# Bilinear MLP, second sweep: the last pair of chunks by seven block products, and a new order table

## The chip, the cores and the metric

The kernel runs on one core of one Trainium2 chip. The metric is the device time of one launch in microseconds (us).

## The reference

```
a   = softmax(phi, over s)                    # phi: 4 x 8 x 576 x 32
k_m = einsum('bhsm,bhsd->bhmd', a, k);  v_m = einsum('bhsm,bhsd->bhmd', a, v)
x   = softmax(q @ k_m.T / 8) @ v_m            # -> 2304 tokens x 512
h   = x @ w_in                                # 512 x 2048
x   = max(0.01*h, h) @ w_out                  # 2048 x 512
out = ((x @ w_a) * (x @ w_b)) @ w_out2        # 512 x 1536, 512 x 1536, 1536 x 512
```

All in fp32. The two MLPs are called the first and the second below.

## The kernel before

Every large product is made of three TensorE passes over fp32r halves (PASSES: high by high, high by low, low by high), so each operand is split: a CAST on ACT (or DVE) makes the high half, a subtraction on DVE the low one.

**Head.** For each batch `b` and group `g` of heads, `kv_part` (L506) loads phi, k and v, takes the maximum of phi on DVE (`nmx`, L490) and the exponential on ACT (L496), transposes it on TensorE (`ta` L543, `tz` L546), copies it out (`en`, L365) and multiplies it with k and v (`km`, L562). The norm `kvn` (L578 on ACT, L580 on DVE) and a transpose `kvt` (L588) follow, and `kd` and `vm` are copied out of it. `sc` (L636) are the scores, `vw` (L719) is v_m by the first chunk of w_in, and `h` (L770) the first product of the first MLP. That chunk comes in four pieces (`raw_win`), which `weight` (L410) takes apart: `high` L429 and `low` L432 on ACT, then clamp L436, shift L440, join L444 and a last addition L447 on DVE. `idle` (L388) places four `warm` transposes (L392), whose result nobody reads, behind a named tile. The first 38 `warm` (L384) run before any data has come.

**Second MLP.** It runs in two sweeps `s` over 12 chunks `c` of 128 of the 1536 columns. `ab_unit` (L1045) makes both factors of one chunk by seven block products of six matmuls each, in three PSUM tiles `abx`, `aby`, `abz` (L1061); ACT copies between them (L1072) and DVE adds (L1069). Two adjacent chunks `2q`, `2q+1` are a pair, and the pair's product with w_out2 is done in one of two ways, as `by_seven(s, c)` (L1126) says from the table `SEVENS`:

- By `o_unit` (L1137): the factors are multiplied (L1093, L1096) and split into `p`. Eight units of six matmuls (L1158), each into a PSUM tile `o` of its own, are added on DVE to the sum `osum` (L1171). In the last pair the eighth unit is cut into 320 and 192 columns. In the last pair each unit is followed by its transfer to the output (L1179).
- By `o_part`: the factors go unsplit into `pf` (L1088, L1091). `p_sums` (L1220) makes T1 to T4 from the blocks B11, B12, B21, B22 by subtraction (L1229), and splits T1 to T4, B11, B21 and B22 into `pb` (CAST L365 on ACT, L1239 on DVE). `w2_sums` (L1185) loads that pair of chunks of w_out2 (L1190) and makes S1 to S4 and their splits from it (L1204, L1214). `o_part` (L1260) then has, for each of two halves `x`, seven parts of three matmuls of 512 columns (L1277). A part is called here by its right operand. B11, T2, T3 and T4 go one after the other into the same PSUM tile `os_x`; B21 goes into `os_y`; T1 and B22 go into `os_z`. After B11, T2 and T3 the running sum in `os_x` is copied out by ACT (`ok`, L1297). After the others DVE adds the tile to `osum` (L1311), and, but for T4, the matching `ok` too (L1314). In the last pair the transfer to the output follows (L1321).

**Order.** `Program.run` (L275) issues the operations in the order of the table `ORDER`: an operation's number, with a letter a (ACT) or v (DVE) where either could do it. Each engine works through its own share strictly in that order. `PLACES` names the buffer of each tile; the tiles `os_x` of all pairs lie in one PSUM bank, those of `os_y` and `os_z` in a second.

Of the kernel before, what the change touches and what calls it, by code (L numbers as in the profile page):

```python
# [58 lines left out]
SEVENS = ((0,1,2,3,8,9,10,11), tuple(range(10)))  # L59
# [30 lines left out]
24 246 0 4 238 1 26 25 224 27 3 28 2 247 29 31 30 231 248 249v 34a 250 32a 251 35 33 45 239 240 241v 23 252v 242 253 5 44 243 6 244v 22 36 7 8 46 226 37 10a  # L90
47 225 245 38v 227v 49 9 11 12a 39 65 13 40a 43v 41a 14 228 42a 232 48 229 15 64 16a 230v 233 17 234v 290 20a 235 21a 19a 18v 257 299 236 259a 237v 258a 87
88 89 254 75 50 255a 256a 76 63 90 51 77 52 91v 98 55 54 78 57a 92 53 66 79 56a 67 68a 93 150 69a 80v 116 58 94v 81 117 70 59v 95 101 82 291 60 326 292 61a
332 62v 115 71a 83v 300 328 327 293v 301 84 99 72 330 333 294 96a 302v 334 73a 295 100 329 74a 303 331 296v 139 85a 317 304 335 336 297a 140 102 308 265
305v 344 266a 168 103 141 267 268a 338 142 306a 127 345 269 337 143v 104 167 128 154 144 106 340 339a 145 155 342 108a 129 156 130 146v 158 131 343a 118 341
147 160a 119 364 121a 120a 132v 169 148a 105 86v 133 157 319 122 149v 318 134 153 260 320v 358 261a 123a 262 310 135v 263a 309 264 136 170 311v 124 151 172a
384 126v 137a 372 125a 138v 365a 107 312 159 390 179 109a 385 313 386 171 321 161a 391 110 314v 173a 373 322 359a 354 152 111a 323v 374 392 112 375v 348
113a 114v 315a 352 324a 316v 356 325v 355 349 387v 350 180 351v 393v 370 357v 298v 307v 181 360 97v 371a 353a 182 366 362 361 183 376 368 367 363v 184v 369v
185 174 377a 186 270 541 382 273a 271a 175a 272 187v 394 383a 274 188 176 532 346 178a 189a 177a 190v 395a 378 505 191 379 380 162 193 347a 192 194 275 550
195v 559 396 276a 278a 277 196 279 388 163a 197 542 414 381v 389a 198v 406 415 199 416 398 544v 200a 417v 164 201v 418 165a 166a 397 543 399v 545 407a 213
533 546 412 215 547v 214 548a 216 202 552 534 402 203 204 419a 217v 413a 408 561 205 403 280 409 206v 218 424 404 281a 405v 410 411v 432 425a 219 283a 436  # L100
434 207 282 208 285 437a 560 284 426 209v 433 288a 430 428 289 507 210 427 286a 211a 287 400 220v 431a 551 212v 420 221 442 429v 498 222a 535v 484 421 223v
491 422 423v 450 443a 435v 506 536 438 562v 451 537 452 444 401a 563 458 553v 446 453v 439 448 440 564 445 459 554 460 538v 441v 462 565v 447v 466 463 555
464 566a 454 556v 467 461v 472 468 455 456 478 557a 457v 567v 539a 470 499 549v 1274 492 1300 540v 1281 473 558v 479 449a 465v 474 469v 485 476 475v 486
508v 480 471a 481v 493 509 501v 500 494v 482 510 477a 1275 502 503 495 487v 496 572 483a 488 1276 489 1301 497v 1302 511v 490v 578 573a 504v 1277v 1303v 512
1278 579a 1304 1279 584 513a 515a 514 1305 590 1280v 516 1292a 1306v 585a 568 1293v 1307 1308a 1282 574 1310 1309v 1283 1284v 1314 522 569 1285 570 1286 575
580 576 1287v 591a 571v 586 581 1288v 1294a 577v 596 582 1289v 587 583v 588 1290v 1296a 1291v 589v 592 1298a 1297v 525a 598 593 1312 523a 602 1315 594 1322
595v 1341 1295v 1299v 604 524 1313 610 605 1311 526 606 608 597a 603 607v 517 609 614 520a 518a 521 1316 519 612 620 611 600 613v 599 601v 615 622 744 1318v
621 616 1319 624 623 626 617 1317 634 618 627 619v 630 1342 1320 628 625v 527 631 629v 632 1321v 644 765 633v 1333v 751 654 792 645 758 636 646 635 530a
528a 1343 529 638 1323 637v 1324 648 531 639 1334v 640 1344v 1351 1325v 647v 1345 641v 650 1326 649 656 651 652 662 653v 1346 660 801 663 1327 657 664 1328v
658 1347v 1335a 655 1348 1349a 668 1329v 746 1331v 1330v 642 1350v 1337a 1336v 1332v 753 661 745 1338v 752 674 665v 1353 759 1352 672 1339a 810 760 1355  # L110
1340v 643 1354 666 659v 675 670 676 669 677v 767 678 667 766 754v 671v 802 747v 793 761v 684 748 794 768v 679 804v 673 680 755 819 795v 690 682 762 811 796
685 681 803 769 813v 686 812 805 814 692 687 691 688 696 689v 694 693 749 756 770 702 820 683v 821 806 797 710 763 704 712 695v 1382 711 698 708 1356 699
700 1363 705 701v 706 697 822v 714 815 718 703 716 715 823 722 707v 719 717v 720 713v 726 723 721v 724 750v 730 727 757v 728 824 709 764v 771v 738 725v 798v
# [180 lines left out]
def tile_mem_attention__leaky_mlp__bilinear_mlp(  # L294
# [1146 lines left out]
```

## Time and profile before

| | |
|---|---|
| median of 3 runs | 777.59 us (776.81 to 779.49) |
| profiled execution | 777.41 us |
| its span, first to last instruction | 775.6 us |
| mean granted TensorE clock | 0.993 |
| TensorE (PE) busy | 767.0 us, 99% |
| VectorE (DVE) busy | 647.7 us, 84% |
| ScalarE (ACT) busy | 402.6 us, 52% |

The profiled execution is 1.81 us longer than its span. Sums are made against the profiled execution, which is 0.18 us under the median. In the timeline a row gives the start and length of a group of like instructions on one engine; a PE group's length reaches to the end of its last matmul and so overlaps the start of the next.

### The profile page before, as it was taken

The page shows a single profiled execution, that of the slowest core. Times are in us where ns is not written, and L with a number is a line of the kernel's source. Part 1 is how long each engine was busy: PE and PEld are TensorE (multiplying, and loading weights), DVE is VectorE, ACT ScalarE, POOL GpSimd, SP SyncE. Part 2 cuts the span into 40 slices and gives each one's busy share as a digit, 9 for nine tenths or more (in the row PEclk, how much of TensorE's full clock was granted, in tenths as well). Part 3 has the DMA queues.
Part 4 walks back from the last instruction along what each step waited for, and adds up shares of the span by engine and source line. Part 5 has one row for each costly group of instructions (what it writes and reads, how often), then busy time and mean ns, then how long its engine had stood idle before and what let it go on. Part 6 is the DMA issues. An engine that isn't in the chain of part 4 may idle for free.

```text
span 775.6 us, 12742 instructions
## 1 busy us (share of the span) xinstructions
PE 767.0 (99%) x4766; PEld 656.8 (85%) x4766; DVE 647.7 (84%) x1249; ACT 402.6 (52%) x866; POOL 0.7 (0%) x6
## 2 busy tenths in 40 slices
PE   7999999999999999999999999999999999999998
PEld 6577898899889978898988888888888888888886
DVE  5897899689877989698685789999999688789877
ACT  5685786675546646654433445644543424444330
POOL 0000000000000000000000000000000000000000
PEclk9799999999999999999999999999999999999999
DMA  9993241665039141635973629775798685765523
GB/s 321 374 323 109 84 164 68 200 235 177 1 129 331 58 144 74 245 109 216 375 268 118 219 82 332 263 256 199 235 339 326 241 314 171 253 244 202 182 105 108
DMA packets 59868, 158.89 MB, mean 205 GB/s; under 512 B 7520, under 2 KB 22880, under 8 KB 59808
## 3 DMA queue, kind: packets, MB, share of 16 engines
q1 hardware_dynamic: 59808, 158.09, 57.6%
q8 instruction: 37, 0.61, 0.3%
q14 instruction: 23, 0.19, 0.1%
HBM read 111.41 MB, written 46.66 MB: 204 GB/s over the span
## 4 chain that ended last, share of the span: by engine, by line
PE 96%; DMA 2%; SPq 0%; DVE 0%; ACT 0%; issue 0%
PE y L840 24%; PE abx L1061 17%; PE h L788 13%; PE abz L1061 8%; PE o L1158 6%; PE os_x L1277 6%; PE aby L1061 4%; PE os_z L1277 3%; PE a L1115 2%; PE b L1115 2%; PE y L836 2%; PE vw L719 2%; PE os_y L1277 2%; DMA phi<-in_phiT_dram 1%; PE km L562 1%; DMA raw_win<-in_w_in_dram 1%
## 5 line engine op out<-in xcount | busy, mean ns | idle before, releaser
L840 PE MATMUL y<-g,wout 128*128 128x320 f32 (+2 forms) x1104 | 198.3, 333 | 0.0
L840 PEld LDWEIGHTS y<-g,wout 128*128 128x128 f32 x1104 | 175.0, 188 | 18.0 <-issue 3.8
L1061 PE MATMUL abx<-yb_T,wo 128*128 128x512 f32 x432 | 110.0, 390 | 0.0
L1061 PEld LDWEIGHTS abx<-yb_T,wo 128*128 128x128 f32 x432 | 80.1, 188 | 16.8 <-ACT t L1072 0.6
L1072 ACT COPY t<-abx 128x512 f32<-128x512 f32 x72 | 42.0, 586 | 61.7 <-PE abx L1061 60.6
L788 PE MATMUL h<-ahi,vwh 128*128 128x320 f32 (+1 forms) x240 | 72.8, 303 | 0.0
L788 PE MATMUL h<-ahi,vwl 128*128 128x320 f32 (+1 forms) x240 | 71.0, 296 | 0.0
L788 PE MATMUL h<-alo,vwh 128*128 128x320 f32 (+1 forms) x240 | 71.0, 296 | 0.0
L804 DVE TENSOR_TENSOR g<-t,g 128x256 fp32r<-128x256 f32 (+1 forms) x120 | 52.6, 452 | 15.9 <-ACT t L741 11.8
L741 ACT ACTIVATE g<-h 128x320 fp32r<-128x320 f32 (+1 forms) x120 | 48.3, 416 | 33.4 <-PE h L788 30.6
L741 ACT ACTIVATE t<-h 128x256 f32<-128x256 f32 (+1 forms) x120 | 49.4, 419 | 26.2 <-PE h L788 24.9
L1297 ACT COPY ok<-os_x 128x512 f32<-128x512 f32 x54 | 31.7, 586 | 58.9 <-PE os_x L1277 52.8
L788 PEld LDWEIGHTS h<-ahi,vwh 128*128 128x128 f32 x240 | 45.4, 189 | 8.0 <-issue 5.0
L859 DVE TENSOR_TENSOR acc<-y,acc 128x320 f32<-128x320 f32 (+1 forms) x72 | 39.3, 552 | 9.7 <-PE y L840 9.5
L788 PEld LDWEIGHTS h<-alo,vwh 128*128 128x128 f32 x240 | 45.5, 189 | 0.6
L788 PEld LDWEIGHTS h<-ahi,vwl 128*128 128x128 f32 x240 | 45.5, 190 | 0.0
L1069 DVE TENSOR_TENSOR t<-abz,t 128x512 f32<-128x512 f32 x48 | 32.9, 685 | 8.7 <-PE abz L1061 5.9
L1061 PE MATMUL abz<-yb_B,wo 128*128 128x512 f32 x144 | 36.7, 390 | 0.0
L1061 PE MATMUL abz<-yb_T,wo 128*128 128x512 f32 x144 | 36.6, 390 | 0.0
L1061 PE MATMUL abx<-yb_B,wo 128*128 128x512 f32 x144 | 36.5, 390 | 0.0
L1061 PE MATMUL aby<-yb_B,wo 128*128 128x512 f32 x144 | 36.5, 390 | 0.0
L1158 PE MATMUL o<-p,wout 128*128 128x512 f32 (+2 forms) x150 | 35.6, 383 | 0.0
(372 smaller groups left out, 1447.6 us busy)
## 6 DMA issues: line engine op xcount, KB each, us to landing
k_wo<-wo SPq DMA_DIRECT2D x24, 512.0 KB, 4.0
wo<-k_wo SPq DMA_DIRECT2D x24, 512.0 KB, 4.6
raw_wout<-in_w_out_dram SPq DMA_DIRECT2D x22, 512.0 KB, 5.4
raw_win<-in_w_in_dram SPq DMA_DIRECT2D x16, 512.0 KB, 6.6
kv<-in_kv_dram SPq DMA_DIRECT2D x16, 512.0 KB, 10.2
wf<-k_wf SPq DMA_DIRECT2D x9, 512.0 KB, 4.4
k_yb_T<-yb_T SPq DMA_DIRECT2D x8, 512.0 KB, 6.3
yb_T<-k_yb_T SPq DMA_DIRECT2D x8, 512.0 KB, 5.8
```

Of the source, the lines that this page charges most:

```text
L741: nc.scalar.activation(dst, src, AF.Prelu, alpha=0.01)
L788: nc.tensor.matmul(T[o], T[w[u]][:, k, fs], T[a[v]][:, k, cols], start=(k == 0 and i == 0), stop=(k == 1 and i == 2))
L804: lambda T, e: engines[e].tensor_tensor(T[g][:, i, 1, to], T[t], T[g][:, i, 0, to].bitcast(F32), op=ALU.subtract),
L840: nc.tensor.matmul(T[o], w[:, u, here], T[g][:, j, v, at:at + m], start=(f == 0 and p == 0), stop=(f == 3 and p == 2))
L859: "DVE", c_dve(m), lambda T: nc.vector.tensor_tensor(T[acc][:, i, :], T[o], T[acc][:, i, :], op=ALU.add),
L1061: nc.tensor.matmul(T[o], T[w][:, which, u, k * P:(k + 1) * P], T[ys[v]][:, k, :], start=first and k == 0 and x == 0, stop=k == 1 and x == ...
L1069: op("DVE", 0.69, lambda T: nc.vector.tensor_tensor(T[to], T[o], T[x], op=ALU.add), r=[o, x], w=[to], tiles=[o, x, to])
L1072: op("ACT", 0.59, lambda T: nc.scalar.copy(T[t], T[X]), r=[X], w=[t], tiles=[X, t])
L1115: nc.tensor.matmul(T[o], T[w][:, k // 2, u, k % 2 * P:(k % 2 + 1) * P], T[ys[v]][:, k, :], start=(k == 0 and x == 0), stop=(k == 3 and x = ...
L1158: nc.tensor.matmul(T[o], T[w][:, u, es], T[g][:, at, v, here], start=(x == 0 and k == 0), stop=(x == 1 and k == 2))
L1277: nc.tensor.matmul(T[o], lhs(T, u), T[g][:, v, :], start=i in (1, 2, 5) and k == 0, stop=k == 2, skip_group_check=True)
L1297: op("ACT", 0.59, lambda T: nc.scalar.copy(T[k][:, x, :], T[o]), r=[o], w=[(k, x)], tiles=[o, k])
```

## The change

In the table that says which chunks go by seven block products, chunks 10 and 11 of the second sweep are added; for this, the order table and the buffer table are set anew from end to end (one line of the order table is shown of each).

```diff
-SEVENS = ((0,1,2,3,8,9,10,11), tuple(range(10)))
+SEVENS = ((0,1,2,3,8,9,10,11), tuple(range(12)))
 ORDER = """
-24 246 0 4 238 1 26 25 224 27 3 28 2 247 29 31 30 231 248 249v 34a 250 32a 251 35 33 45 239 240 241v 23 252v 242 253 5 44 243 6 244v 22 36 7 8 46 226 37 10a
+24 246 0 4 238 1 26 25 27 224 3 28 29 30 2 32a 247 33 249v 231 31 250 34a 248 35 45 239 240 23 241v 242 251 44 5 6 22 7 8 243 46 226 36 225 10a 47 227v 37 9
...
```

The lines of the changed kernel stand three further down than before (L1277 is L1280 there). In its tail, the last pair's 54 matmuls of L1158 (eight units, the eighth in two cuts) become 42 of L1280 (14 parts of three). `w2_sums` and `p_sums` now run for this pair too, with one more load of 512 KB, and the outputs leave by L1324.

**ACT in the head.** Rows of ACT from the first exponential on, before (`en` are the copies of the transposed phi, `cv_win` the conversion of w_in):

```order
L496 ACTIVATE phi_1_93,es_78<-phi_1_93,nmx_77 128x576
L429 ACTIVATE cv_win_3_154<-raw_win_3_95 128x512
L432 ACTIVATE cv_win_3_154<-raw_win_3_95 128x512
L365 COPY en_1_169<-tz_1_158 64x128
L365 COPY en_1_169<-ta_1_160 128x512
L429 ACTIVATE cv_win_2_185<-raw_win_2_138 128x512
L432 ACTIVATE cv_win_2_185<-raw_win_2_138 128x512
L496 ACTIVATE phi_0_140,es_78<-phi_0_140,nmx_77 128x576
```

and now:

```order
L499 ACTIVATE phi_1_93,es_78<-phi_1_93,nmx_77 128x576
L368 COPY en_1_161<-ta_1_154 128x512
L432 ACTIVATE cv_win_3_163<-raw_win_3_95 128x512
L368 COPY en_1_161<-tz_1_172 64x128
L435 ACTIVATE cv_win_3_163<-raw_win_3_95 128x512
L432 ACTIVATE cv_win_2_184<-raw_win_2_138 128x512
L435 ACTIVATE cv_win_2_184<-raw_win_2_138 128x512
L499 ACTIVATE phi_0_140,es_78<-phi_0_140,nmx_77 128x576
```

The two conversions of `cv_win_3` stood ahead of both copies of `en_1`; now the larger copy stands ahead of both of them, and the smaller one between them. The exponential of `phi_0` stands behind the same rows as before.

**PE in the head.** Rows of PE from the first transposes on, before:

```order
L546 MATMUL tz_1_158<-ident,phi_1_93 64x128
L543 MATMUL ta_1_160<-ident,phi_1_93 128x128 x4
L562 MATMUL km_1_174<-kvr_136,en_1_169 32x128 x4
L392 MATMUL warm<-ident,en_1_169 128x128 x4
L392 MATMUL warm<-ident,cv_win_3_154 128x128 x4
L562 MATMUL km_1_174<-kv_1_0_144,en_1_169 32x128 x8
L543 MATMUL ta_0_215<-ident,phi_0_140 128x128 x4
L562 MATMUL km_1_174<-kv_1_1_142,en_1_169 32x128 x8
L392 MATMUL warm<-ident,cv_win_2_185 128x128 x4
L546 MATMUL tz_0_246<-ident,phi_0_140 64x128
L392 MATMUL warm<-ident,en_0_232 128x128 x4
```

and now:

```order
L546 MATMUL ta_1_154<-ident,phi_1_93 128x128 x4
L395 MATMUL warm<-ident,en_1_161 128x128 x4
L549 MATMUL tz_1_172<-ident,phi_1_93 64x128
L565 MATMUL km_1_177<-kvr_136,en_1_161 32x128 x4
L546 MATMUL ta_0_200<-ident,phi_0_140 128x128 x4
L565 MATMUL km_1_177<-kv_1_0_144,en_1_161 32x128 x8
L565 MATMUL km_1_177<-kv_1_1_142,en_1_161 32x128 x8
L549 MATMUL tz_0_232<-ident,phi_0_140 64x128
L591 MATMUL kvt_1_240<-ident,kvn_1_234 128x128 x2
```

`ta_0`, which needs the exponential of `phi_0`, stood behind the products with `kv_1_0`; now it stands ahead of both products with `kv_1`. Three of the four groups of `warm` rows have gone from here to places further down. The fourth stands ahead of `tz_1`.

**PE in the tail.** Rows of PE from the last product `abz` of chunk 11 (its last row shown) to the end, before (`os_4` is pair 4 of the chunks, `o_10` the last pair):

```order
L1061 MATMUL abz_11_8236<-yb_B_0_1_6734,wo_11_3_8126 128x512
L1277 MATMUL os_4_1_z<-pb_4_B_8102,w_1_4_1_8055 128x512 x3
L1158 MATMUL o_10_0_0_8307<-p_10_0_8245,wout_10_1_8121 128x512 x3
L1158 MATMUL o_10_0_0_8307<-p_11_0_8293,wout_11_1_8146 128x512 x3
L1158 MATMUL o_10_0_1_8316<-p_10_0_8245,wout_10_1_8121 128x512 x3
L1158 MATMUL o_10_0_1_8316<-p_11_0_8293,wout_11_1_8146 128x512 x3
L1158 MATMUL o_10_0_2_8328<-p_10_0_8245,wout_10_1_8121 128x512 x3
L1158 MATMUL o_10_0_2_8328<-p_11_0_8293,wout_11_1_8146 128x512 x3
```

and so on in sixes to the end. Now, from behind that `abz` on (`os_5` is the last pair, `os_5_0` and `os_5_1` its two halves):

```order
L1280 MATMUL os_4_1_x<-pb_4_T_8114,w_1_4_0_8061 128x512 x3
L1280 MATMUL os_4_1_z<-pb_4_T_8016,w_1_4_0_8061 128x512 x3
L1280 MATMUL os_4_1_x<-pb_4_T_8128,w_1_4_1_8087 128x512 x3
L1280 MATMUL os_4_1_x<-pb_4_T_8167,wout_9_1_8048 128x512 x3
L1280 MATMUL os_4_1_z<-pb_4_B_8104,w_1_4_1_8087 128x512 x3
L1280 MATMUL os_5_0_x<-pb_5_B_8198,wout_10_1_8175 128x512 x3
L1280 MATMUL os_5_0_y<-pb_5_B_8300,wout_11_1_8156 128x512 x3
L1280 MATMUL os_5_0_x<-pb_5_T_8324,w_1_5_0_8260 128x512 x3
L1280 MATMUL os_5_0_z<-pb_5_T_8257,w_1_5_0_8260 128x512 x3
L1280 MATMUL os_5_0_x<-pb_5_T_8347,w_1_5_1_8222 128x512 x3
L1280 MATMUL os_5_0_x<-pb_5_T_8332,wout_11_1_8156 128x512 x3
L1280 MATMUL os_5_0_z<-pb_5_B_8329,w_1_5_1_8222 128x512 x3
```

The half `os_5_1` follows with the same seven parts, its last two the other way round: `os_5_1_z` from `pb_5_B`, then `os_5_1_x` from `pb_5_T`, which is the last of all. Four parts of pair 4 stood ahead of that last `abz` and stand behind it now, beside the one that stood behind it already, and 14 parts follow in which `os_x` comes eight times.

## Rows read from the trace of the kernel before

**Rows 1.** The page, busy time, share of the span and instructions of each engine

```profile
PE 767.0 (99%) x4766; PEld 656.8 (85%) x4766; DVE 647.7 (84%) x1249; ACT 402.6 (52%) x866; POOL 0.7 (0%) x6
```

**Rows 2.** Stretches: length, busy us of PE, PEld, DVE, ACT, POOL, PEclk, DMA share, GB/s

```profile
17.40:21.10 3.70, 1.97 (x35) 0.87 (x36) 3.14 (x7) 2.73 (x8) 0.00 (x0) 1.00 1.07 387
21.10:25.60 4.50, 3.93 (x47) 0.76 (x33) 3.25 (x6) 1.59 (x5) 0.00 (x0) 0.50 1.04 284
25.60:31.40 5.80, 5.80 (x70) 3.96 (x74) 5.07 (x13) 3.38 (x8) 0.00 (x0) 0.50 1.03 391
31.40:755.00 723.60, 723.60 (x4412) 624.79 (x4404) 612.62 (x1183) 383.64 (x824) 0.00 (x0) 1.00 0.57 202
...
772.60:775.60 3.00, 0.00 (x0) 0.00 (x0) 0.34 (x1) 0.00 (x0) 0.00 (x0) 0.98 0.47 156
```

**Rows 3.** Chain that ended last, 3 to 26 us: start us, us, what

```profile
3.95 0.45 SPq L526
...
13.63 9.61 DMA phi<-in_phiT_dram
...
23.26 1.36 DVE nmx L490
...
24.65 0.88 ACT phi L496 x2
```

**Rows 4.** Timeline of ACT, 6 to 19 us: start us, us, what, idle before and releaser

```profile
6.11 0.67 ACT L429 ACTIVATE cv_win<-raw_win 128x512 f32<-128x512 f32 x1 [0.23 <-DMA raw_win<-in_w_in_dram]
...
9.26 0.58 ACT L365 COPY en<-ta 128x512 f32<-128x512 f32 x1 [0.18 <-PE ta L543]
...
12.52 0.77 ACT L496 ACTIVATE phi<-phi,nmx 128x576 f32<-128x576 f32 x1 [1.53 <-DVE nmx L490]
...
18.13 0.45 ACT L578 ACTIVATE kvn<-km,er 128x256 f32<-128x256 f32 x1
```

**Rows 5.** Timeline of DVE, 11 to 32 us, same columns

```profile
11.74 0.74 DVE L490 TENSOR_REDUCE nmx<-phi 128x1 f32<-128x576 f32 x1
...
31.07 0.70 DVE L680 STREAM_TRANSPOSE at<-sm 128x512 f32<-128x512 f32 x1
```

**Rows 6.** Timeline of PE, 8 to 33 us, same columns

```profile
8.63 0.60 PE L543 MATMUL ta<-ident,phi 128*128 128x128 f32 x4
...
13.44 0.66 PE L543 MATMUL ta<-ident,phi 128*128 128x128 f32 x4 [0.49 <-ACT phi L496]
...
16.30 1.08 PE L562 MATMUL km<-kv,en 128*32 128x128 f32 x32
18.64 0.44 PE L588 MATMUL kvt<-ident,kvn 128*128 128x128 f32 x2 [1.25 <-ACT kvn L578]
...
28.09 1.94 PE L562 MATMUL km<-kv,en 128*32 128x128 f32 x32
...
32.54 0.81 PE L770 MATMUL h<-at,vwf 128*128 128x256 f32 x3
```

**Rows 7.** Timeline of PE, 755 us to the last matmul

```profile
755.71 0.84 PE L1277 MATMUL os_x<-pb_T,w 128*128 128x512 f32 x3
...
759.11 1.52 PE L1061 MATMUL abz<-yb_B,wo 128*128 128x512 f32 x6
760.47 0.84 PE L1277 MATMUL os_z<-pb_B,w 128*128 128x512 f32 x3
761.15 11.39 PE L1158 MATMUL o<-p,wout 128*128 128x512 f32 x54
```

**Rows 8.** Timeline of ACT, the last ok copies

```profile
756.59 0.59 ACT L1297 COPY ok<-os_x 128x512 f32<-128x512 f32 x1 [0.77 <-PE os_x L1277]
```

**Rows 9.** Timeline of DVE, 747 us to its end

```profile
747.72 0.69 DVE L1096 TENSOR_TENSOR t<-t,t 128x512 f32<-128x512 f32 x1
...
757.12 1.28 DVE L1314 TENSOR_TENSOR osum<-osum,ok 128x512 f32<-128x512 f32 x2
...
772.58 0.36 DVE L1171 TENSOR_TENSOR osum<-o,osum 128x192 f32<-128x192 f32 x1 [0.34 <-PE o L1158]
```

More of the change, by code (lines that the diff above doesn't have):

```diff
@@ L94 @@
[L94 to L101, printed above, removed]
@@ new lines @@
+1384 735v 834 833 1383 742 842 1360 836 1361 835 1366v 1362v 1385v 850 841 743 1374v 856 851 1367 837v 843v 828 1386 857 1368 858 830 829 844 782 845 1369v
+846 831v 838 848 847 783a 849v 1375v 864 839 1392 784 852 777 853 859 854 1376a 855v 862 1370v 860 785a 1387 865 1388v 780a 868 778a 1371v 1389 863 866
+1390v 874 1373v 861v 1372v 1391v 786 1396 870 779 880 1397 871 781 1378a 867v 872 1380a 1379v 876 1377v 1394 1423 882 873v 877 1381v 1404 878 886 883 881
+1395 884 890 1393 885v 879v 894 869 892 887 891 787 888 889v 893v 898 875 1004 788a 1011 790a 789 904 1018 791 908 905 906 899 907v 895 900 1398 896 914
@@ new lines @@
+1248 1500v 1515 1254 1582a 1516 1258 1247 1251 1249v 1264 1260 1493v 1245v 1632 1494v 1631 1495v 1501a 1496v 1583v 1503a 1256 1502v 1517 1262 1257 1504v
+1552a 1566a 1518 1565v 1568 1605 1253 1259 1255v 1557v 1603 1261v 1263 1553v 1270 1567v 1604 1265 1569 1677 1559v 1554a 1584a 1606 1594a 1586 1585v 1633
+1555v 1561v 1587 1266 1607 1272 1267 1595v 1271 1563v 1268 1273 1655 1592a 1610 1602 1269 1680 1556v 1608 1574a 1576 1575v 1618 1609 1722 1612 1577 1634
+1679 1558v 1560v 1570a 1619 1578a 1572 1571v 1678 1613 1620a 1562v 1573 1611 1636 1588a 1656v 1621 1635 1579v 1615 1622a 1637 1614 1658v 1616 1649 1638 1723
@@ new lines @@
+1623v 1624a 1617v 1785 1625v 1639 1626v 1589v 1641 1640 1627a 1724 1628v 1644 1580 1581 1643 1590 1657v 1591 1650 1593v 1660a 1725 1651a 1642 1703 1661v
+1682 1704 1646 1683 1684 1647 1645 1689 1648v 1652 1659v 1653a 1664v 1727 1670a 1662v 1665a 1675a 1685 1666v 1663v 1671v 1707 1784 1686 1597 1667v 1705
+1654v 1668a 1687 1669v 1672v 1708 1698 1676v 1673a 1688 1674v 1709 1706 1786 1692 1596 1710 1691 1690 1711 1713 1712a 1694 1728 1714 1748 1715 1749 1693
+1730 1695 1717a 1718v 1752 1696v 1697 1753 1719v 1731 1729 1699a 1700 1720v 1732 1701a 1716 1721v 1734 1733 1735 1750 1739 1681 1751 1736 1754 1702v 1758
@@ new lines @@
+1861 1839 1862 1865v 1869 1843 1840 1917 1842 1870 1872 1868v 1846 1890v 1891v 1903 1874 1812v 1898a 1946 1875 1899v 1853 1918 1905v 1832 1847 1893v 1942
+1947 1900a 1984 1813v 1958 1920 1943 1873v 1914 1901v 1944 1848v 1949 1906 1921 1948v 1851a 1919 1907 2045 1904 1965 1950 1986 2038 1924 1945 1985 1788
+1852v 1833 1855a 1959 1844 1987v 1988 1908v 1952 1926 1909 1910a 1915 1922 1953 1989 1911v 1854 1990v 1961v 1991 1992a 1951v 1956 1923 1993v 1966 1937 1925
+1998 1967 1962 1960 1963 1954 1845 1927 1964v 1968v 1976a 1929 1856 1849a 1969 1955 1857a 1957 1936 1850v 2064 1858v 1930 2024 2039 1977v 2026 1970 1994
@@ new lines @@
+f7 b4 b4 s12 g6 f0 s10 s22 s10 s18 g3 f1 g0 b0 b6 b5 t2 t3 t1 s6 b3 b3 b4 s3 b3 f1 s13 s23 f1 g3 s2 g1 s4 s13 s11 s9 s11 b7 b0 b2 t0 t4 t2 s9 f7 g4 b3 b4 b3
+f0 g6 s17 s20 s12 s8 f4 g7 s4 s22 b1 b5 b0 t1 t3 t0 s16 b3 b4 s8 b3 f4 g4 s9 s2 s8 g0 f7 s4 g7 s3 s10 s13 s7 s10 b2 b7 b6 t2 t3 t4 s7 b3 b4 b3 s11 g6 s9 s18
+f0 s18 s6 g3 s3 s6 b2 b7 b5 t3 t4 t2 s12 b3 b4 s2 b3 g4 f4 g1 f1 s5 s21 s26 f7 g3 s17 s13 s23 s20 s16 b6 b5 b0 t0 t3 t4 g1 b3 b4 b3 f2 g0 s20 g6 s17 b3 b4
+s19 b3 s27 s12 b3 b4 b3 b3
```

227 lines of the change are left out of this document (109 added, 118 removed).

## The prediction

> **What bounds the kernel now.** The page's first part comes first: TensorE is busy for 767.0 of 775.6 us [rows 1], so 8.6 us of idle time is all there is. The table of stretches shows where it lies: from 31.40 to 755.00 PE is busy for 723.60 of 723.60 us, and after the last matmul it is idle for 3.00 [rows 2]. About 5.5 us lie in the first 26 us; the longest wait there for other work is 1.25 us, of the transposes `kvt` for a norm on ACT [rows 6]. So the middle can only change by PE work, the head by waits and by the clock, and the tail by both. For the clock see the same table: 1.00 up to 21.10, 0.50 (the lower level, 1.2 GHz) from there to 31.40, after a stretch in which PE did 1.97 of 3.70 us [rows 2]. The chain of waits says that the head hangs on a transfer at first: the phi of the next batch lands at 23.24, DVE takes its maximum, ACT its exponential to 25.53 [rows 3], and PE works without a break from then on.
>
> **The change, part by part.** Its time is the profiled execution, 777.41, plus the terms.
>
> *Tail, PE work.* From the last product `abz` (759.11) a product of six matmuls takes 1.36 and a part of three 0.68, as the next rows' starts show; the 54 matmuls of L1158 run for 11.39, of which 0.15 is the drain of the last, so 11.24 [rows 7]. They go: −11.24. Fourteen parts come: +14 × 0.68 = 9.52. Net **−1.7**.
>
> *Tail, waits of PE.* In before each unit had a PSUM tile of its own. Now `os_x` is written, copied out by ACT and written again. A part starts at 755.71 [rows 7] and its copy at 756.59 for 0.59 [rows 8]: 0.88 and 0.59, and with 0.06 for the handing over (the norm on ACT ends at 18.58 [rows 4], `kvt` behind it starts at 18.64 [rows 6]) the next part into `os_x` may start 1.53 after the one before. With nothing between, PE is ready after 0.68 and waits 0.85; with one part between it is ready after 1.36 and waits 0.17. On the changed order's list of parts I count two of the first kind (T3 to T4 in pair 4 and in the first half of pair 5) and four of the second: 2 × 0.85 + 4 × 0.17 = 2.4. Two more waits are for DVE, which must take T4 out of `os_x` before B11 of the next half begins: 0.88 and 0.69 and 0.06 after T4's start, against 1.36, so 0.27 by itself; and DVE has a queue by then. Taking each addition at 0.60 where it follows an independent one, and 0.69 where not (two in 1.28; one alone 0.69) [rows 9], and DVE's order as it stands, I get 0.27 and 0.60. The same walk gives 0.29 for T2 of the first half (its low half is a chain of addition, product, two subtractions, cast and subtraction behind the last `abz`) and 0.37 for the last B22, whose tile `os_z` waits for DVE. Sum **+3.9**. Lower bound 2.4, if DVE's queue never counts; upper bound 4.5, if each of the ten waits also bares a weight load, at some 0.06.
>
> *Tail, the end.* Before, the last addition ends at 772.94 [rows 9], and the span 2.7 later, the transfer among it. In the walk the last matmul ends at 18.4 after the start of `abz`; DVE has two additions left then, to 19.8, and the second of two transfers is issued some 0.45 (an issue in the chain) [rows 3] behind the first: 19.8 + 0.45 + 2.7 = 23.0. That is 4.7 behind the last matmul against 3.00 [rows 2]: **+1.7**. Checked as a whole: before, from 759.11 to 775.6 is 16.49; now 23.0, of which four parts of pair 4, 2.72, were formerly ahead of `abz`; 23.0 − 16.49 − 2.72 = 3.8. The three terms give 3.9. The two additions per part beyond the old ones, the casts and the sums of w_out2 stand on ACT and DVE beside PE's products; where they do not fit they are in the waits above. The added 512 KB load falls in a stretch with a DMA share of 0.57 [rows 2] and is costed at nothing; if it were late, the S parts would be, by some tenths.
>
> *Tail against the skill.* Parts into `os_x` with copies after them stand in 31.40 to 755.00 too, and PE lost nothing to them [rows 2]; by that alone the waits would be 0 and the tail −1.7 + 1.7 = 0. The Trainium skill ("Perfetto Trace Analysis", Matmuls) says that independent groups of matmuls should go round different PSUM banks, so that the copying out of one lies beside the next group's matmuls; here the parts share one bank and nothing else stands between, and by that rule the 3.9 is real. I go by the starts and copies of [rows 7, 8].
>
> *Head, conversions.* The larger copy of `en_1`, at 9.26 after PE's transpose at 8.63 [rows 4, 6], now stands ahead of the conversions of `cv_win_3`, which ran at 6.11 in time that was ACT's to spare [rows 4]. They start at about 9.6 and push DVE's two clamps, two shifts and a join, and behind them the maximum of `phi_0`, from 11.74 [rows 5] to about 13.3, its exponential from 12.52 [rows 4] to 14.05, and `ta_0` from 13.44 [rows 6] to 14.97: +1.53. PE has put the products that filled this time behind `ta_0`, so it idles from about 10.6 to 15.0. Everything behind goes later: `km` from 16.30 [rows 6] to some 17.9, the transposes behind the norm by 1.4, the scores by 1.3. PE was idle for some 0.5 before the next batch's transposes, waiting for the phi that lands at 23.24 [rows 3]; that takes up 0.5 of the 1.3, and a group of `warm` now stands just there, 0.66 at the full clock and some more at half. From there to `h` at 32.54 [rows 6] PE is busy for all of 5.80 us [rows 2], so the delay stays: **+1.5**, if the clock falls and rises with the work as it did.
>
> *Middle.* The order is changed in single places, the PE work is the same, PE had not one wait there [rows 2], and DVE has 111 us to spare in it. I take 0, bounds −0.1 (no wait is left to gain) and +0.6.
>
> Sum: −1.7 + 3.9 + 1.7 + 1.5 = 5.4; 777.41 + 5.4 = **782.8**.
>
> **The rivals.**
> *The clock falls in the new gap.* PE idles for 4.4 us at 10.6 to 15.0; before, a stretch with 1.97 of 3.70 us was followed by half clock for 10 us [rows 2]. For it: the new gap is emptier than that one. At half clock a `km` group takes 1.94 in place of 1.08 [rows 6]. The work of 15 to 21, 5 us, would take some 4 longer; waits for ACT take up one or two of that, and if the clock rises before 31.4, up to 2.9 of the 5.80 comes back. Head +3.5 by my walk: 777.41 + 3.9 + 3.5 = 784.8, with +1.5 to +5 as its ends. The skill ("TensorE: Matmul & The Clock Gate", Part 1) has the throttled state as the default, which activity releases and idling brings back; by that rule this rival is the one. The traces have one fall only, at 21.1, and none behind the idle 1 us pieces of 10 to 13.
>
> *Not slower: the clock holds through 31.4.* The `warm` groups that moved from 10 to 15 now stand at some 19, 22 and 26, where PE was half idle before. If that keeps the clock at 1.00, the 5.80 us at half clock [rows 2] become some 2.9. Then `at` on DVE, at 31.07 [rows 5] and now rid of a norm of 0.48 ahead of it, bounds `h` at about 30.95 in place of 32.54: head −1.6. 777.41 + 3.9 − 1.6 = 779.7, within 0.3%. It decides at 21: clock 1.00 or not in 21 to 31. Against it: the added rows are 2 us in all, and the gap before is larger.
>
> *The waits of the tail don't come:* the rows of before have none. 777.41 + 0 + 1.5 = 778.9. Against it: the ACT copy must end before the next part begins, in any trace.
>
> *The order's long middle loses or gains unseen:* up to 3 us to either side, small chance, as PE had no idle time there.
>
> **How the numbers follow.** Forecast 0.52, clock falls early 0.22, clock holds 0.14, no waits in the tail 0.07, middle 0.05. A measurement of this kernel can tell about 0.3%, 2.3 us: 775.3 to 779.9 is the same. Slower: the forecast, the early fall and 0.03 of the last: 0.77. The same: 0.10 of the clock that holds and 0.06 of the tail without waits, 0.16. Faster: 0.04 of the clock that holds, 0.01 of the tail without waits, 0.02 of the middle: 0.07. Range: lower end where the clock holds (779.7) and the tail is a little kinder, 779.5; upper end 777.41 + 4.5 + 5 = 786.9, so 787. Out of it lie the 0.07, 0.05 of the clock that holds, 0.04 of the middle and 0.03 above: 0.19.
>
> **What would show it.** PE's waits: `os_x` at L1280 for `ok` on ACT, two of 0.85 and four of 0.17, and for DVE 0.3 and 0.6; from `abz` to the end of the span 23.0. `ta_0` at 15.0, a gap of 4.4 before it, `h` at 34.1, clock 0.50 in about 22 to 33. The middle busy to the last 0.1. Wrong if PE runs on through the last 14 parts without a wait, if `h` starts before 32.5, or if the clock falls before 20.

## The result and the profile after

The changed kernel took 784.80 us in the median of 4 runs (783.99 to 785.75), the kernel before 777.73 beside it: 1.0084 times as long, with an interval of 1.0062 to 1.0105. That is 7.1 us slower by the medians, and 6.5 by the ratio. The forecast was 782.8, its range 779.5 to 787.0. The profiled execution of the changed kernel took 784.07, with a span of 782.0, and is thus 0.7 under its median.

The page's first part, as in [rows 1]: PE is busy as long as before, for a longer span. The instructions are 12 fewer, the 54 matmuls that became 42.

```profile
PE 767.7 (98%) x4754; PEld 653.3 (84%) x4754; DVE 657.5 (84%) x1264; ACT 411.3 (53%) x880; POOL 0.7 (0%) x6
```

The table of stretches, cut at the places where this trace changes (columns as in [rows 2]):

```profile
10.60:15.00 4.40, 1.16 (x8) 0.84 (x12) 3.07 (x8) 2.67 (x7) 0.00 (x0) 0.62 1.03 409
15.00:21.10 6.10, 5.75 (x78) 3.78 (x79) 4.36 (x9) 3.19 (x9) 0.00 (x0) 0.50 1.07 379
...
25.60:31.40 5.80, 5.05 (x93) 3.01 (x87) 5.66 (x11) 4.25 (x12) 0.00 (x0) 1.00 1.04 399
...
36.00:757.00 721.00, 721.00 (x4369) 621.69 (x4368) 614.41 (x1185) 383.33 (x820) 0.00 (x0) 1.00 0.57 201
757.00:778.00 21.00, 18.64 (x70) 11.59 (x68) 20.18 (x34) 7.99 (x14) 0.00 (x0) 1.00 0.17 60
778.00:782.00 4.00, 0.00 (x0) 0.00 (x0) 0.65 (x2) 0.00 (x0) 0.00 (x0) 0.71 0.61 211
```

The reader sees three things. The clock is at half in 15.00 to 21.10 and full in 25.60 to 31.40, where before it was the other way round. The middle is busy without a break. And in the last 21 us PE has work for 18.64 while VectorE is busy for 20.18; after the last matmul 4.0 us and more go by.

PE's waits (what waited, for whom, us in total, times, longest): two rows, one in the head, where it was 0.5 before, and one in the tail, where before had none.

```profile
PE ta L546 <- ACT phi L499: 3.8, 1, 3.8
...
PE os_x L1280 <- ACT ok L1300: 1.4, 2, 0.7
```

The head, as ScalarE shows it (start, length, what, idle time before and its releaser), to be held against [rows 4]: the copy at 7.86 stands ahead of the conversion, and the exponential of phi_0 comes at 12.91.

```profile
7.86 0.59 ACT L368 COPY en<-ta 128x512 f32<-128x512 f32 x1 [2.15 <-PE ta L546]
8.35 0.68 ACT L432 ACTIVATE cv_win<-raw_win 128x512 f32<-128x512 f32 x1
...
12.91 0.77 ACT L499 ACTIVATE phi<-phi,nmx 128x576 f32<-128x576 f32 x1 [1.66 <-DVE nmx L493]
```

And as PE shows it, against [rows 6]:

```profile
7.23 0.60 PE L546 MATMUL ta<-ident,phi 128*128 128x128 f32 x4
...
13.84 1.11 PE L546 MATMUL ta<-ident,phi 128*128 128x128 f32 x4 [3.80 <-ACT phi L499]
14.88 1.94 PE L565 MATMUL km<-kv,en 128*32 128x128 f32 x32
...
29.66 1.08 PE L565 MATMUL km<-kv,en 128*32 128x128 f32 x32
...
33.09 2.76 PE L773 MATMUL h<-at,vwf 128*128 128x256 f32 x12
```

The second `ta` waited 3.80 us. The `km` group behind it takes 1.94, at half clock; the next batch's `km` group takes 1.08 at 29.66, at the full clock, where the same one took 1.94 before [rows 6]. The first `h` is at 33.09, 0.55 later than before, although PE had started 1.4 earlier: the first `ta` is at 7.23 against 8.63, since the 38 `warm` rows before it went at the full clock from 4.8 on here and from 7.5 on there. With the clock back by 25.60, another thing sets the first `h`; the chain that ended last (start, length, what) runs through VectorE, with a maximum of phi and the softmax of the first scores, and then through the norm on ScalarE:

```profile
25.29 1.24 DVE nmx L493
26.53 0.60 DVE mx L669
...
28.71 0.82 DVE mx L669
...
32.28 0.48 ACT kvn L581
```

The tail on PE, from the last product `abz` on, against [rows 7]:

```profile
758.29 1.52 PE L1064 MATMUL abz<-yb_B,wo 128*128 128x512 f32 x6
759.65 0.84 PE L1280 MATMUL os_x<-pb_T,w 128*128 128x512 f32 x3
...
761.17 0.96 PE L1280 MATMUL os_x<-pb_T,w 128*128 128x512 f32 x3
762.81 0.96 PE L1280 MATMUL os_x<-pb_T,wout 128*128 128x512 f32 x3 [0.68 <-ACT ok L1300]
763.61 0.86 PE L1280 MATMUL os_z<-pb_B,w 128*128 128x512 f32 x3
764.55 0.97 PE L1280 MATMUL os_x<-pb_B,wout 128*128 128x512 f32 x3
...
770.30 0.85 PE L1280 MATMUL os_z<-pb_B,w 128*128 128x512 f32 x3
771.26 0.97 PE L1280 MATMUL os_x<-pb_B,wout 128*128 128x512 f32 x3
...
776.31 0.88 PE L1280 MATMUL os_x<-pb_T,wout 128*128 128x512 f32 x3
```

And what the parts wait for, on ScalarE and on VectorE (its last addition stands there too) and SyncE's transfers:

```profile
762.17 0.59 ACT L1300 COPY ok<-os_x 128x512 f32<-128x512 f32 x1 [1.05 <-PE os_x L1280]
```

```profile
763.81 0.69 DVE L1314 TENSOR_TENSOR osum<-os_x,osum 128x512 f32<-128x512 f32 x1
...
777.97 0.68 DVE L1317 TENSOR_TENSOR osum<-osum,ok 128x512 f32<-128x512 f32 x1
```

```profile
770.63 8.97 SPq L1324 DMA_DIRECT2D out_dram<-osum  x12
```

T3 into `os_x` starts at 761.17, its copy runs from 762.17 to 762.76, T4 starts at 762.81: 1.64 apart, where a part takes 0.68. Then VectorE takes T4 out from 763.81 to 764.50, and B11 starts at 764.55, where PE would have been ready at 764.29. A part that starts after a wait is listed with 0.96, one that follows without a break with 0.84: its first weight load is no longer beside other matmuls, and the next part starts 0.80 behind it in place of 0.68. The weight loads of T4 show it: they start at 762.81, with its matmuls, after the same wait.

```profile
762.81 0.53 PEld L1280 LDWEIGHTS os_x<-pb_T,wout 128*128 128x128 f32 x3 [1.11 <-ACT ok L1300]
```

From 759.65 to 776.31 there are 18 parts, 12.24 us at 0.68; the starts are 16.66 apart, so PE lost 4.4 us. From the start of `abz` to the end of the span are 23.7 us.

### The profile page after: what moved, and what is told of

It reads as the page before. It is cut to its first block, busy times and chain, and to the rows that moved or that the text cites. A ratio compares the mean times of both kernels' runs of the same rounds, so it can differ in the third digit from the quotient of the medians.

```text
span 782.0 us, 12754 instructions
## 1 busy us (share of the span) xinstructions
PE 767.7 (98%) x4754; PEld 653.3 (84%) x4754; DVE 657.5 (84%) x1264; ACT 411.3 (53%) x880; POOL 0.7 (0%) x6
## 4 chain that ended last, share of the span: by engine, by line
PE 96%; DVE 2%; ACT 1%; issue 0%; DVEq 0%; POOLq 0%; POOL 0%; ACTq 0%
PE y L843 24%; PE abx L1064 17%; PE h L791 13%; PE abz L1064 8%; PE os_x L1280 7%; PE o L1161 5%; PE aby L1064 4%; PE os_z L1280 3%; PE a L1118 2%; PE b L1118 2%; PE vw L722 2%; PE y L839 2%; PE os_y L1280 2%; PE km L565 1%; PE h L773 1%; PE warm L387 1%
## 5 line engine op out<-in xcount | busy, mean ns | idle before, releaser
L744 ACT ACTIVATE g<-h 128x256 fp32r<-128x256 f32 (+1 forms) x120 | 48.4, 416 | 46.4 <-PE h L791 44.9
L1300 ACT COPY ok<-os_x 128x512 f32<-128x512 f32 x60 | 35.2, 588 | 66.0 <-PE os_x L1280 58.6
L807 DVE TENSOR_TENSOR g<-t,g 128x320 fp32r<-128x320 f32 (+1 forms) x120 | 52.5, 451 | 14.7 <-ACT t L744 11.1
L1072 DVE TENSOR_TENSOR t<-abz,t 128x512 f32<-128x512 f32 x48 | 32.9, 685 | 12.4 <-PE abz L1064 9.3
L1280 PE MATMUL os_x<-pb_T,w 128*128 128x512 f32 x120 | 33.9, 395 | 0.0
```

Of the source, the lines that this page charges most:

```text
L744: nc.scalar.activation(dst, src, AF.Prelu, alpha=0.01)
L807: lambda T, e: engines[e].tensor_tensor(T[g][:, i, 1, to], T[t], T[g][:, i, 0, to].bitcast(F32), op=ALU.subtract),
L1072: op("DVE", 0.69, lambda T: nc.vector.tensor_tensor(T[to], T[o], T[x], op=ALU.add), r=[o, x], w=[to], tiles=[o, x, to])
L1280: nc.tensor.matmul(T[o], lhs(T, u), T[g][:, v, :], start=i in (1, 2, 5) and k == 0, stop=k == 2, skip_group_check=True)
L1300: op("ACT", 0.59, lambda T: nc.scalar.copy(T[k][:, x, :], T[o]), r=[o], w=[(k, x)], tiles=[o, k])
```

## The experiments

The first column of times is the median, the ratio is to the runs of before taken beside it, and the last four are read in each trace: the start of the first `h` and the time from there to the end of the span, and the same for the first `abz`, with which the second MLP starts.

| run | median us | ratio (95% interval) | first h | first h to end | first abz | first abz to end |
|---|---|---|---|---|---|---|
| before | 777.6 | | 32.5 | 743.1 | 365.3 | 410.3 |
| the change | 784.8 | 1.0084 (1.0062 to 1.0105) | 33.1 | 748.9 | 366.9 | 415.1 |
| e1 tail alone | 782.0 | 1.0052 (1.0034 to 1.0070) | 34.3 | 747.8 | 367.0 | 415.1 |
| e2 head alone | 779.7 | 1.0020 (1.0011 to 1.0029) | 32.6 | 743.9 | 366.1 | 410.3 |
| e3 six banks | 783.1 | 1.0069 (1.0052 to 1.0086) | 33.0 | 749.3 | 367.0 | 415.4 |
| e4 six additions out | 784.3 | 1.0081 (1.0064 to 1.0098) | 32.9 | 748.5 | 366.8 | 414.7 |
| e5 both | 781.6 | 1.0056 (1.0039 to 1.0073) | 33.6 | 746.3 | 367.5 | 412.4 |
| e6 head to first h | 779.7 | 1.0027 (1.0008 to 1.0047) | 34.5 | 743.2 | 367.4 | 410.3 |
| e7 head, maximum early | 777.8 | 1.0003 (0.9991 to 1.0015) | 32.0 | 743.7 | 365.4 | 410.3 |
| e8 before, maximum early | 777.9 | 1.0010 (0.9999 to 1.0020) | 32.5 | 745.0 | 365.4 | 412.1 |
| e9 GpSimd | 782.5 | 1.0053 (1.0035 to 1.0070) | 32.1 | 748.8 | 365.0 | 415.9 |
| e10 change, maximum early | 783.2 | 1.0069 (1.0049 to 1.0090) | 31.6 | 748.7 | 365.0 | 415.3 |
| e11 two queues | 780.5 | 1.0039 (1.0026 to 1.0052) | 33.6 | 746.3 | 366.3 | 413.5 |
| e12 fillers moved | 778.0 | 1.0002 (0.9992 to 1.0012) | 31.9 | 743.3 | 364.9 | 410.3 |

The first `h` moves by some 2 us from run to run of one kernel (e1 has the head of before, and its profiled run was its slowest by 2 us). The last column is free of that: with the tail of before it is 410.3 in five of six traces, with that of the change 415.1 to 415.3 in three. The traces of e3, e8 and e9 have waits for late operands in the second MLP besides (1.0 to 1.1 us by the view of waits): from the first to the last `abz` they take 1.7, 1.7 and 2.1 us longer than e5, before and e11, which issue the same order there. With that taken off, the last column is 413.7 for e3 and 413.9 for e9, and the tails are compared by it. The heads are compared by the medians: with the head of before the first `abz` starts anywhere between 365.0 and 367.0.

**e1 and e2: the tail alone, the head alone.** Wherever both order tables have done the same set of operations, one can be cut and the other go on.

```diff
 e1: SEVENS of the change
-ORDER = change[0:2775] + change[2775:]
+ORDER = before[0:2775] + change[2775:]
 e2: SEVENS of before
-ORDER = before[0:324] + before[324:]
+ORDER = change[0:324] + before[324:]
```

> The order and buffers of before up to the first products of pair 2 of the second sweep, those of the change from there on: the tail alone. My theory (PE waits in the last parts, a longer end): +4.6 against before, 782.3, with eight to ten waits of PE on L1280, and a head with the clock at 0.50 in about 21 to 31 as before. Rival (the tail is nearly free, the loss is the head's): +1 or less, 778.7.

> The order and buffers of the change for its first part, up to about 92 us, those of before behind it, with the last pair by o_unit: the head alone. My theory (the copies ahead of the conversions delay ta_0, PE idles for some 4 us, the clock falls there and comes back earlier): +1.4 to +2.5 against before, 779.1 to 780.2; clock 0.50 in about 12 to 21 and 1.00 from 22. Rival (the early rise of the clock pays for the gap): within 0.5 of before, 777.2 to 778.2.

Measured: e1 782.0, +4.3; e2 779.7, +2.0. Both theories stand, both rivals fall. Together they make 6.3 of the 7.1; the other 0.8 is less than the intervals are wide. By the last column, the tail costs 4.8 in both the change and e1.

**e6: the head up to the first `h`.**

```diff
-ORDER = before[0:129] + before[129:]
+ORDER = change[0:129] + before[129:]
```

> The order of the change only up to the first h (about 33 us), that of before behind it. My theory (the loss of the head comes in about equal parts before and behind the first h; the traces give 0.5 and 0.8): +0.6 to +1.3 against before, 778.3 to 779.0. Rival (all of it lies behind the first h): 777.4 to 778.0. Rival (all of it before): 779.4 to 779.9.

Measured: 779.7, as much as e2. That is what the second rival forecast, all of the head's loss before the first `h`, and above my theory of two equal parts; the interval (0.6 to 3.7 us over before) does not quite shut the theory out. The 0.8 that I read behind the first `h` does stand in the traces: from there to the first `abz` the seven with the change's order take 333.3 to 333.9 us, the seven with that of before 332.7 to 333.0. But e2, which has it, is no slower than e6, which has not. This trace also happens to be the one that compares with before's, since its first `ta` is at 8.38 against 8.63. Its PE timeline:

```profile
8.38 0.60 PE L542 MATMUL ta<-ident,phi 128*128 128x128 f32 x4
...
14.99 1.12 PE L542 MATMUL ta<-ident,phi 128*128 128x128 f32 x4 [3.81 <-ACT phi L495]
...
34.49 2.76 PE L769 MATMUL h<-at,vwf 128*128 128x256 f32 x12
```

The first `h` is at 34.49 against 32.54 [rows 6]: +1.95, near the +2.3 of the medians.

**e3, e4, e5: the bank, the additions, both.** For e3 the buffer table gives the six tiles of the last pair banks of their own, and the order table puts the parts of its two halves between each other (the buffers are shown); e4 leaves out the additions of the kept sums in the last pair; e5 does both.

```diff
 e3: PLACES, for os_5_0 x, y, z and os_5_1 x, y, z
-b4 b3 b3  b4 b3 b3
+b1 b2 b7  b5 b6 b0
 e4: o_part, the addition of ok
-lambda T, e: engines[e].tensor_tensor(into(T), into(T), T[k][:, x, :], op=ALU.add),
+lambda T, e: None if s and q == NC2 // 2 - 1 else engines[e].tensor_tensor(into(T), into(T), T[k][:, x, :], op=ALU.add),
```

> The change, with the tiles os_x, os_y, os_z of the last pair's two halves in six PSUM banks that are free by then, and the parts of the two halves put between each other, so that no part needs a tile just read. If the shared bank is the whole loss: PE's waits in the tail, 4.4 us, go and so does the time, -4.4 against the change, 780.4. If VectorE is the bound just behind it (busy for 20.2 of 21.0 us in 757 to 778): PE's waits go but the time falls by 2.0 at most, 782.8, and the span ends 6 to 7 us behind the last matmul.

> The change, with the six additions of the kept sums (L1317) of the last pair left out: the output lacks them. They are 6 x 0.60 = 3.6 us of VectorE's work in the last 20 us; PE's waits for the copies on ACT stay. If the shared bank sets the pace: -0.3 to -0.7 against the change, 784.1 to 784.5. If VectorE sets it: -2 to -3.6, 781.2 to 782.8.

> The third and the fourth experiment in one: six banks with the halves put between each other, and the six additions of the kept sums of the last pair left out (the output lacks them). If the shared bank and VectorE's work each hide behind the other: more than the sum of the two (-1.7 and -0.5 against the change), -3.5 to -4.1, 780.7 to 781.3. If they are two separate costs: -2.2, 782.6.

Measured: e3 783.1, -1.7 against the change; e4 784.3, -0.5; e5 781.6, -3.2. The ratios, each to its own runs of before, make that -1.2, -0.2 and -2.2, with intervals that overlap. The traces tell more: from the first `abz` to the end the three are -1.4 (with e3's late operands taken off), -0.4 and -2.7 against the change. So neither limit alone gives much back, and both together more than their sum, a little less than I had expected. Of the tail's 4.8, e5 leaves 2.1 that no run takes away. The stretches of e3:

```profile
757.00:775.00 18.00, 17.91 (x78) 14.22 (x77) 17.81 (x30) 7.69 (x14) 0.00 (x0) 1.00 0.06 21
775.00:782.40 7.40, 0.00 (x0) 0.00 (x0) 4.30 (x8) 0.00 (x0) 0.00 (x0) 0.81 0.65 232
```

Up to 775 PE now has hardly a gap, and its last matmul ends at 774.9 where it had been 777.2. But VectorE is busy for 17.81 of 18.00, and has 4.30 us of work left when PE has none. Its timeline there, four additions in a row and the last one:

```profile
772.01 2.49 DVE L1314 TENSOR_TENSOR osum<-osum,ok 128x512 f32<-128x512 f32 x4
...
778.61 0.69 DVE L1311 TENSOR_TENSOR osum<-os_x,osum 128x512 f32<-128x512 f32 x1
```

In e4 it is the other way round. The last 21 us:

```profile
757.00:778.00 21.00, 18.50 (x69) 11.44 (x68) 17.42 (x28) 7.99 (x14) 0.00 (x0) 1.00 0.21 75
```

VectorE falls from 20.18 to 17.42 there, and PE's busy time, 18.64 in the change, stays at 18.50.

**e9: the additions on GpSimd; e11: two queues for the output.** e9 has the order of before up to the tail, and then a tail like e3's, in the same six banks, in which seven additions of kept sums carry the letter g. e11 is e9 with half of the twelve output transfers issued by ScalarE.

```diff
 e9: ORDER
-3034v 3037v 3042v 3064v 3067v 3095v 3106v
+3034g 3037g 3042g 3064g 3067g 3095g 3106g
 e11: o_part, the transfer
-nc.sync.dma_start(
+(nc.scalar if at or (w_ == 512 and x) else nc.sync).dma_start(
```

> The order of before up to pair 2 of the second sweep, and behind it the tail of the third experiment (six banks, halves put between each other), with seven of the additions of kept sums (L1317) of the last two pairs given to GpSimd, which is idle. If VectorE's queue is what is left of the loss: by a walk with 2.45 us for one addition on GpSimd the tail is as long as before's, 777.2 to 778.2. If GpSimd's additions are late or slow VectorE down: PE or VectorE wait for them, 779.5 to 782.

> The ninth experiment with six of the last pair's twelve output transfers issued by ScalarE, which has nothing left to do by then, in place of SyncE. There the twelve issues follow each other from 772.3 to 778.0, 0.48 apart, and the last lies 0.7 behind VectorE's last addition. If SyncE's issuing is the third limit of the tail: -0.7 to -1.1 against the ninth experiment, 781.4 to 781.8. If the transfers themselves share one path: unchanged, 782.2 to 782.8.

e9 measured 782.5, where e1, with the same head, had 782.0: a miss. (By its trace, with the late operands taken off, its tail is 1.2 shorter than that of e1; the medians do not show it.) The additions on GpSimd are no longer VectorE's, but some of VectorE's own became slower while GpSimd worked. Three operations of e9 on VectorE, a subtraction beside GpSimd's addition, one behind it, and an addition beside GpSimd's next, and those additions (four pieces each):

```profile
762.12 0.94 DVE L1230 TENSOR_TENSOR pf<-pf,pf 128x512 f32<-128x512 f32 x1
...
764.73 0.68 DVE L1215 TENSOR_TENSOR w<-w2s,w 128x512 fp32r<-128x512 f32 x1
765.33 0.68 DVE L1312 TENSOR_TENSOR osum<-os_y,osum 128x512 f32<-128x512 f32 x1
```

```profile
761.19 3.07 POOL L349 TENSOR_TENSOR osum<-osum,ok 128x128 f32<-128x128 f32 x4 [2.27 <-ACT ok L1298]
765.27 4.82 POOL L349 TENSOR_TENSOR osum<-osum,ok 128x128 f32<-128x128 f32 x8 [1.01 <-ACT ok L1298]
```

The subtraction took 0.94 beside GpSimd (761.19 to 764.26), the one behind it 0.68, and the addition at 765.33, which reads the PSUM tile `os_y`, 0.68 although GpSimd works. So it is in the whole tail of e9: of the eleven operations of this size that run beside GpSimd (for 0.39 us or more) and read SBUF alone seven took 0.90 to 0.95, and all thirteen that read a PSUM tile 0.68 to 0.69. The seven make some 1.8 us. At the end, SyncE issues all twelve transfers one after the other, for 5.71 us, until 777.98; VectorE's last addition had ended at 776.86.

```profile
772.27 5.71 SPq L1322 DMA_DIRECT2D out_dram<-osum  x12
```

With ScalarE issuing six of them (e11), SyncE's six are out by 776.46:

```profile
771.52 4.94 SPq L1322 DMA_DIRECT2D out_dram<-osum  x6
```

e11's ratio is 1.0039 against 1.0053 for e9, about 1.1 us less, but the two intervals overlap (1.0026 to 1.0052, 1.0035 to 1.0070). The traces do not settle it either: of the 2.4 us that e11 is shorter from the first `abz` to the end, 2.1 are e9's late operands ahead of the last `abz`, and from there to the end it is 22.4 against 22.7. SyncE is done 0.8 earlier against the last `abz`, and the span ends only 0.3 earlier. That the issuing limits this tail is thus not shown. Neither comes near before.

**e7, e8, e10: the maximum of phi_0 earlier.** Two numbers of the order table go ahead of the conversions of `cv_win_2`: in the head of e2 (e7), in before (e8), in the change (e10).

```diff
 e7, e10
-... 248 35 45 239 240 23 241v 242 251 44 5 6 22 ...
+... 248 35 45 5 6 239 240 23 241v 242 251 44 22 ...
 e8
-... 45 239 240 241v 23 252v 242 253 5 44 243 6 ...
+... 45 5 6 239 240 241v 23 252v 242 253 44 243 ...
```

> The second experiment (head of the change, rest of before) with the maximum and the exponential of phi_0 put ahead of the conversions of cv_win_2 on VectorE and ScalarE; phi_0 has landed at 9.4 there. My theory (the gap of 4 us before ta_0 is that maximum's place in VectorE's queue, and it is what the head loses): the gap falls to 1.5 or less, the clock stays at 1.00 to 15 at least, and the time falls by 1 to 2 against the second experiment, 777.7 to 778.7. Rival (the head is set by later work, and by the clock wherever it falls): the gap goes, the time stays at 779.3 to 780.

> The kernel before with the same move alone: the maximum and the exponential of phi_0 ahead of the conversions of cv_win_2. If PE's first products set the time of the first h: ta_0 from 13.4 to about 11.5, -0.5 to -1.5 against before, 776.2 to 777.2. Rival (the phi of the next batch, landing at 23, and the half clock behind it set it): within 0.3 of before, or slower where the clock falls earlier.

> The whole change with the maximum and the exponential of phi_0 put ahead of the conversions of cv_win_2, as in the seventh experiment. If head and tail add up: -1.9 against the change, 782.9. Rival (the gain of the seventh experiment belongs to its other rest): 784 to 785.

e7 measured 777.8, 1.9 under e2 and level with before; `ta_0` comes at 11.76 after a wait of 1.52 in place of 3.8:

```profile
11.76 0.87 PE L542 MATMUL ta<-ident,phi 128*128 128x128 f32 x4 [1.52 <-ACT phi L495]
```

So the place of that one maximum in VectorE's queue, with the exponential that waits for it, accounts for what the head lost, to within e7's interval of some 1 us to either side, whatever else was moved there. The expected clock was wrong, though: it fell at 12.1 all the same, rose at 15.5 and fell once more from 22.3 to 25.7.

e8 measured 777.9, no gain, but it is no test of an earlier `ta_0`. In the order of before a group of `warm` and a group of `km` stand ahead of `ta_0`, and the `warm` group waits for a conversion that the maximum and the exponential now push back, so `ta_0` came later than the 13.44 of before:

```profile
12.63 0.91 PE L391 MATMUL warm<-ident,cv_win 128*128 128x128 f32 x4 [2.75 <-DVE cv_win L446]
...
14.48 1.12 PE L542 MATMUL ta<-ident,phi 128*128 128x128 f32 x4
```

e10 measured 783.2, 1.6 under the change, close to the 1.9 of e7. The intervals of e10 and of the change overlap, so the times alone do not settle it; in the trace the first `abz` starts 1.9 earlier than in the change, and the tail is as long (415.3 against 415.1). That head and tail add up is likely, then, and not settled.

**e12: fillers moved and doubled in before.**

```diff
-FILL = 4
+FILL = 8
 ORDER
-... 225 245 38v 227v 49 9 11 12a ... 229 15 64 16a 230v 233 17 234v ...
+... 225 38v 227v 49 9 12a ... 229 15 11 64 16a 230v 233 17 245 234v ...
```

> The kernel before with two of its four groups of warm rows moved into PE's idle time at 17.4 to 20 (one behind the products ahead of that idle time, one behind the transposes kvt), and eight transposes to a group in place of four. If they keep the clock at 1.00 in 21 to 31: the first h at about 31, -1 to -1.6 against before, 776.1 to 776.7: a version that beats both. If the clock falls all the same: +0.3 to +1 for the added rows, 777.9 to 778.6.

Measured: 778.0, no difference. The clock did hold. Its stretches:

```profile
21.10:25.60 4.50, 2.48 (x48) 0.67 (x33) 3.24 (x6) 1.72 (x5) 0.00 (x0) 1.00 1.04 268
25.60:31.40 5.80, 4.13 (x89) 2.78 (x89) 5.60 (x13) 3.18 (x8) 0.00 (x0) 1.00 1.03 393
```

Yet the first `h` came only at 31.88. PE's timeline shows why: it waits for the exponential of the next phi, and for the loads of kv.

```profile
25.45 0.30 PE L545 MATMUL tz<-ident,phi 128*64 128x128 f32 x1 [1.56 <-ACT phi L495]
...
28.86 0.64 PE L561 MATMUL km<-kv,en 128*32 128x128 f32 x16 [0.86 <-DMA kv<-in_kv_dram]
...
31.88 1.46 PE L769 MATMUL h<-at,vwf 128*128 128x256 f32 x6
```

The trace of e9 says the same without any new filler. Its head has the order of before and its first `ta` starts at 8.43, close to before's 8.63; its clock was at 0.50 from 13.9 to 17.3 and at 1.00 from there on, and its first `h` came at 32.1 against 32.5, the first `abz` at 365.0 against 365.3. Its stretch:

```profile
25.60:31.40 5.80, 4.03 (x82) 2.77 (x82) 5.70 (x14) 3.62 (x10) 0.00 (x0) 1.00 1.03 376
```

## Why the prediction was right, and where it was not

The direction, the size and the two places were right; the range held the time. One of its own signs of being wrong came true, though: the clock fell before 20, at 11.6. The forecast had kept the clock as it was, so in the head what came is the early fall that a rival had. That the rival's time, 784.8, is the measured median to the digit is luck: it had 3.5 for the head, where about 2.0 was measured, and 3.9 for the tail, where 4.3 to 4.8 was. By its steps:

*Tail, PE work, -1.7:* right. 12 matmuls fewer, and every product and part without a wait has the durations of [rows 7].

*Tail, waits of PE, +3.9:* measured 4.4. The two waits between T3 and T4 are there, and the waits for VectorE. Two sizes in it were off, and they work against each other. A part behind a wait bares 0.12 of weight load, so the starts lie 1.64 apart in place of 1.53; the 3.9 had nothing for this, and only its upper bound had 0.06 a wait, which no row gave. Against that, the second B11 waits 0.28 for VectorE (770.30 to 771.26, less 0.68), where the walk had 0.60.

*Tail, the end, +1.7:* measured 4.8 against 3.1 from the last matmul to the end of the span, +1.7. Whole tail by the trace: 23.7 - 16.5 - 2.7 = +4.5; e1 gives +4.3.

*What the 3.9 is made of.* I wrote that by the Trainium skill's rule on banks ("Perfetto Trace Analysis", Matmuls) the 3.9 is real, and that the row without waits would make it nothing. The trace agrees with the rule as far as PE's waits go: banks of their own, with the two halves' parts put between each other, leave PE busy for 17.91 of 18.00 (e3). But the time does not come back with them. The step that failed is the sentence that what does not fit beside PE's products "is in the waits above": VectorE was full besides, at 20.18 of 21.00. The sum was right because these two limits lie on top of each other, not because PE's waits are the cause alone. What holds the end with both taken away, 2.1 of the tail's 4.8, stays open; that it is SyncE's issuing is not shown (e11).

*Head, +1.5:* measured +2.0 (e2) and +2.3 (e6) by the medians. `ta_0` was forecast for 14.97 and came at 14.99 in e6, the trace with a like start; PE's gap before it was forecast at 4.4 and its wait is 3.8. The cause is the one named: the maximum behind the conversions (e7, e10).

*The clock.* Forecast was half clock in about 22 to 33. It fell at 11.6 and was back at 21.9, in e6 at 14.0 and 24.2. That is the early fall of the first rival, which stood at 0.22, and it agrees with the Trainium skill ("TensorE: Matmul & The Clock Gate", Part 1), by which idling brings the throttled state back. That the new gap made the clock fall is not shown, however: it fell at 12.1 in e7, where the gap is 1.5, and at 13.9 in e9, in the order of before with no wait over 1.0 there. The rival's price was wrong: +3.5 was forecast with up to 2.9 given back, and 2.0 was measured for everything. The stretch of 25.6 to 31.4 ran at the full clock, and the first `h` then hung on VectorE.

*The rival on the other side, the clock that holds:* its condition was tried by itself in e12. With 1.00 up to 31.4 the first `h` came at 31.9 and not at 30.95, for the next phi and the loads of kv were late, and the median did not move. Its -1.6 was too much.

*Middle, 0:* e1 and e2 leave 0.8 of the 7.1 over. The trace of the change has 1.3 us more than before's between the first `h` and the last `abz`, counting the four parts that moved. Of these 1.0 lie ahead of the first `abz`, where e2 has 0.8 of them, and the 0.3 behind it stand in e1 too. That leaves 0.3 at most for the new order of the middle itself, by the traces; no run took the middle by itself.

## What to carry to other kernels

Fewer matmuls do not help where they turn one chain of independent tiles into parts that are each read before the next may start: at the end of a program nothing stands between them. Before giving the last stage a scheme that needs more additions, look at how full VectorE is in that stage alone, not over the span; and when one limit is removed without effect, remove the next with it before discarding the first. In a head that hangs on a chain, the place of one short operation in an engine's queue can be worth as much as all the rest of the order (e7); moving it earlier helps only if nothing else in the queues that follow then waits longer (e8).

## What the runs showed of the hardware that I had not expected

- An addition or subtraction of 128 x 512 on VectorE that takes 0.68 can take 0.90 to 0.95 while GpSimd adds tiles of 128 x 128. In e9 this met seven of the eleven that read SBUF alone and none of the thirteen that read a PSUM tile.
- The 38 `warm` matmuls at the start, the same in every kernel, are done at 8.5 to 8.7 in three traces (before, e6, e9) and at 7.1 to 8.0 in the eleven others: the clock rises at 7.0 to 7.5 in the three and at 4.2 to 6.1 in the others. This moves the first `ta` between 6.9 and 8.6, whatever the order.
- The granted clock at 1.00 up to 31.4 (e12, and e9 from 17.3 on) was worth nothing measurable in that stretch: it waits for loads and for the work that hangs on them.
